# A recurrent attention layer with a feed-forward block: the list of steps after the opening rewritten in another order, transfers as they were

## The chip, the cores and the metric

The kernel runs on one core of one Trainium2 chip. The metric is the device time of one execution in microseconds (us), lower is better. The core has five engines that run side by side, each in its own order: PE (matrix multiply), DVE (vector), ACT (activations), POOL (general purpose) and SP, which here only issues transfers. An engine that waits at one instruction holds back all that stand behind it in its order.

## What is computed

For 4 batches, 8 heads, 768 positions and a head size of 48 a state of 48x48 per head is decayed and updated at each position, and read by `r`; then a normalised feed-forward block with a residual follows.

```python
for t in range(S):
    cur = np.einsum('bhd,bhe->bhde', u[None] * kt, vt)
    y[:, :, t] = np.einsum('bhd,bhde->bhe', rt, state + cur)
    state = w[None, :, :, None] * state + np.einsum('bhd,bhe->bhde', kt, vt)
...
xn = (x - mu) / np.sqrt(var + 1e-06) * g_ln        # x: y as [4, 768, 384]
out = x + np.maximum(xn @ w_ch1, 0.0) @ w_ch2      # 384 -> 1536 -> 384
```

## The kernel before

The 4x768 positions are cut into 24 chunks of 128, six to a batch, numbered 0 to 23. Inside a chunk the recurrence becomes matrix products; between chunks a state Z is carried. The feed-forward block takes chunks in groups: groups 0 to 7 hold one chunk each, groups 8 to 13 two each (chunks 8 to 19), groups 14 to 17 one each.

Nothing is scheduled by the compiler. `PLAN` (line 18) is one list of some 750 steps `name,index,engine`; the loop at its end (line 750) issues them in that order, and each engine runs its own steps in the order of the list. The letter is the engine: `v` DVE, `s` ACT, `g` POOL; `-` is PE for matrix products and SP for transfers. Waits between engines follow from which tile a step reads and writes. Buffers in PSUM are few: `hp` 2 and `at` 2 (two banks each), `y` 1 and `o` 1; a new user of one waits until the last user's reader is done.

The steps that matter, with the chunk or pair or group as index:

- `LK`, `LR`, `LV` (lines 352, 355, 358) load one chunk of k, r, v, 192 KB each, `LK2`, `LR2`, `LV2` (371, 374, 377) a pair of chunks; all are issued by SP.
- `SK`, `SR`, `SR2` multiply k and r by powers of w (through the helper at line 205) on DVE or POOL. `TRk`, `TRr` (400) transpose the result on PE, copied out by `TCk`, `TCr`; `TDk`, `TDr` (423, 428) transpose it by a transfer on SP instead. `CV2` casts v.
- `Q2` (helper, 205) multiplies the transposed tiles of a pair; `AT` (544) forms a chunk's 128x128 products per head, `AM` (553) masks them on DVE. `AT2`, `AM2` and `Y2` (504) are the same for the first four chunks.
- `S` (460 to 481) makes a chunk's share of the state and, for the first of a pair, a per-head factor in the tile `y`; `CC2` and `ZU` (565, or 205 at a batch's first chunk) read it out, `ZD` decays it, `VB2` (492) multiplies v by the factor.
- `Y` (575, 583) makes the chunk's output in the same tile `y`, from the state before, from AM and from v; `X` (590) adds `VB2`'s result. So S, ZU and CC2, Y, X take turns on one buffer.
- `SQ`, `XN`, `RS` are the normalisation. `LT` with `XT` (631, 202) transposes on PE, `LTD` (623) by a transfer on SP.
- `SW` (342 ACT, 344 DVE, 346 POOL) scales and casts one of nine pieces of the first weight, `w_f` to `w_sb`; `IW2` (349) loads the second weight on POOL's queue.
- `UP` (646) is four blocks of 128 (or two of 256) of the first feed-forward product into `hp`, `RL` (662 ACT, 664 DVE) the rectifier; `DN` (674) is a third of the second product into `o`, `OT` (730) adds the residual, `STO` (740) stores. For a one-chunk group, UP's index is 16 times the group plus the weight's third: `UP,2` needs pieces SW 6, 7 and 8.
- `DU` (279) is products of zeros for nothing, a filler of PE's time; `DU,512` is one of them.

The last chunk's second product is done in two halves (`DA`, `DB`, `OA`, `OB`, `SA`, `SB`).

Of the kernel before, what the change touches and what calls it, by code (L numbers as in the profile page):

```python
# [18 lines left out]
WF,0,s MP,1,g LK2,0,- MW,0,v ML,0,v MM2,0,g DU,3072,- UF,0,- TL,0,s MO,0,v MZ,0,v LR2,0,- LR2,1,- MP,2,g MP,0,g LK2,1,-  # L19
LN,0,s MI2,0,g MP,5,g MP,3,g WBM,0,- MP,4,g LG,0,- MM,0,g LV2,0,- DU,4096,- UWR,0,v FR2,0,s MI,0,g FR2,1,s LR2,2,- SRH,0,v  # L20
FK2,0,s SRH,1,v FK2,1,s SKH,0,v LK,5,- FK,0,s TRr,0,- SKH,1,v DU,1024,- TCr,0,s SR2,1,v TRk,0,- LR2,3,- DU,512,- SK2,1,v COL,0,-
TCk,0,s TRr,1,- LV2,1,- CV2,0,s UW,0,v Q2,0,v AT2,0,- DU,1536,- FR,0,s TCr,1,v LK,4,- WL,0,s SR2,2,g AM2,0,v S,0,- AT2,1,-
LK,6,- CC2,0,s DU,512,- ZU,0,v TRk,1,- AM2,1,v DU,512,- VB2,0,g S,1,- TCk,1,s LK,7,- DU,512,- TRr,2,- LW1,1,- SR2,3,v DU,512,-
Y2,1,- TCr,2,s LW1,2,- LV,5,- Q2,1,v Y2,0,- SK,4,g ZU,1,v UGC,0,s LV,4,- CV2,1,s X,1,v TRr,3,- SK,5,g X,0,v DU,512,-
AT2,3,- TCr,3,s DU,512,- AM2,3,v SK,7,g S,2,- XN,1,s AT2,2,- XN,0,g CC2,1,v ZU,2,v SQ,1,s DU,512,- VB2,1,g TRk,2,- AM2,2,v
S,3,- LW1,0,- TCk,2,s DU,512,- SK,6,v LT,1,- Y2,2,- SQ,0,s SW,5,g XT,1,v SW,3,s LV,6,- LT,0,- SW,4,v TRk,3,- Q2,2,g
# [6 lines left out]
DN,2,- RS,2,g LT,5,- S,7,- OT,0,v RL,66,s UP,49,- XN,6,s XT,5,v UP,50,- RL,49,v TCr,4,s LR2,6,- DN,4,- ZU,7,v UP,80,-
ZD,7,v LK,10,- CV2,4,g RL,50,v Y,7,- RL,80,s DN,5,- X,7,v LV,13,- DN,6,- Q2,4,v XN,7,s UP,65,- SQ,4,s OT,1,v LV,11,-
AT,8,- SQ,6,s SR2,6,v AT,9,- DN,8,- RS,6,s LR2,5,- AM,8,v RS,4,s DN,9,- SQ,7,s LK,11,- S,8,- DN,10,- ZU,8,v LV,10,-
UP,82,- CC2,4,s OT,2,v VB2,4,g LK,12,- LT,6,- AM,9,v Y,8,- RL,82,s DN,12,- STO,0,- RL,65,s SK,10,g DN,13,- XT,6,v LK,13,-
X,8,v DN,14,- ZD,8,g LV,12,- S,9,- UP,96,- OT,3,v SK,11,g ZU,9,v UP,98,- RL,96,s SR2,5,v Y,9,- TDk,5,- SQ,8,s DN,16,-
CV2,5,v LT,7,- TRr,5,- SK,12,v DN,17,- X,9,v TCr,5,s RL,98,v LK,15,- UP,97,- XN,9,g LK,14,- XT,7,v ZD,9,g UP,81,- RL,97,s
LR2,7,- XN,8,s SK,13,g UP,112,- RL,81,s LTD,8,- DN,18,- RS,7,s Q2,5,v TRr,6,- OT,4,v UP,114,- SK,15,g TCr,6,s RL,112,v STO,1,-
S,10,- CV2,6,g DN,20,- CC2,5,s TDk,6,- RL,114,s SK,14,v AT,10,- RS,5,s AT,11,- ZU,10,v DN,21,- SR2,7,g AM,10,v UP,113,- STO,3,-  # L40
DN,22,- AM,11,v RL,113,s TDk,7,- Y,10,- VB2,5,g UP,129,- OT,5,v TRr,7,- RL,129,s LR,19,- UP,130,- ZD,10,g X,10,v UP,133,- LV,14,-
Q2,6,v RL,130,s DN,24,- TCr,7,v STO,2,- S,12,- DN,25,- CC2,6,s LV,15,- XN,10,s VB2,6,g ZU,12,v AT,12,- SQ,9,s AT,13,- STO,5,-
AM,12,v Y,11,- RL,133,s DN,26,- Q2,7,g LK,16,- X,11,v UP,128,- OT,6,v XN,11,s Y,12,- UP,131,- X,12,v LK,17,- DN,28,- AM,13,v
SR,19,g CV2,7,s S,13,- DN,29,- LTD,9,- ZU,13,v SQ,12,s DN,30,- ZD,13,g RL,128,s Y,13,- OT,7,v AT,15,- SQ,11,s LR2,8,- AT,14,-
X,13,v UP,132,- STO,4,- SK,17,g RL,131,v SQ,13,s LR,18,- S,14,- AM,15,v LV,17,- XN,13,s DN,32,- LV,16,- XN,12,s DN,33,- ZU,14,v
# [12 lines left out]
UP,210,- AM,21,v RL,208,s DN,64,- SR,22,v S,20,- RL,210,v UP,212,- TDr,11,- CC2,10,v DN,65,- SK,22,v VB2,10,g ZU,20,v DN,66,- Y,20,-
TDk,11,- OT,16,v UP,209,- X,20,v DN,68,- RL,209,s ZD,20,v STO,14,- S,21,- XN,20,g RL,212,v CV2,11,s DN,69,- LTD,14,- ZU,21,v SQ,20,s
DN,70,- UP,213,- RS,13,s OT,17,v STO,16,- UP,211,- STO,15,- Y,21,- RL,211,s DN,72,- X,21,v DN,73,- Q2,11,v SQ,21,s AT,23,- ZD,21,v  # L60
RL,213,s AT,22,- XN,21,v S,22,- LTD,15,- UP,224,- ZU,22,v AM,22,v DN,74,- ZD,22,g RL,224,s UP,226,- CC2,11,s RS,14,s OT,18,v VB2,11,g
# [721 lines left out]
```

## Time and profile before

| | |
|---|---|
| time, median of 3 runs | 149.87 us (149.41 to 149.96) |
| span of the profiled execution, first to last instruction | 147.5 us |
| busy PE / DVE / ACT / POOL | 141.5 / 112.3 / 82.4 / 72.0 us |
| granted PE clock over the span | 1.000 |
| moved by transfers | 27.18 MB, 80338 of 85097 packets under 512 B |

The profiled execution's own time isn't listed; its span is 2.4 us less than the median of the runs, which is what lies around it (149.87 - 147.5). Matrix products are pipelined and their ends are modelled, so "busy" on PE does not mean that it lost nothing: what a product costs in a row of them is read from one start to the next. The view in order of time has, in this order, the start, the time, the engine and line, the operation, the tile written and those read, the shapes and the number of instructions merged; in brackets stands the idle time before it and what ended it. In the windows view stand the engines' busy time in each stretch, the granted clock, the share of time in which the 16 transfer engines were busy (it goes above 1 where packets overlap) and GB/s.

### The profile page before, as it was taken

Reading aid. Unit: us, or ns where it says so; the run is one execution under the profiler, and the core shown is the slowest. Engines: PE = TensorE matmul, PEld = TensorE weight load, DVE = VectorE, ACT = ScalarE, POOL = GpSimd, SP = SyncE. Lnnn points to the kernel's source line nnn. Section 1 sums busy time; section 2 is a strip of 40 time slices with the busy share of each in tenths; the row PEclk is TensorE's granted clock in tenths of the full one; section 3 lists DMA queues with packets and bytes.
Section 4 is the critical chain, followed back from the end, with each engine's and each line's share of the span. In section 5 each row is a group of like instructions: output and inputs, shape, how many; then the busy total and the mean of one; then the engine's idle time right before and its main releaser. Section 6 shows DMA issues by size and latency. Waiting matters only on the chain.

```text
span 147.5 us, 4689 instructions
## 1 busy us (share of the span) xinstructions
PE 141.5 (96%) x1943; PEld 111.1 (75%) x1943; DVE 112.3 (76%) x206; ACT 82.4 (56%) x181; POOL 72.0 (49%) x96
## 2 busy tenths in 40 slices
...
GB/s 112 300 242 240 192 339 187 283 243 215 220 95 231 202 225 165 264 205 258 164 192 196 195 235 124 173 204 227 197 112 191 182 142 154 82 46 119 8 99 111
DMA packets 85097, 27.18 MB, mean 184 GB/s; under 512 B 80338, under 2 KB 83540, under 8 KB 85076
## 3 DMA queue, kind: packets, MB, share of 16 engines
...
q8 instruction: 15, 0.25, 0.7%
...
q10 hardware_dynamic: 2, 0.00, 0.0%
HBM read 18.88 MB, written 4.72 MB: 160 GB/s over the span
## 4 chain that ended last, share of the span: by engine, by line
PE 65%; SPq 13%; DMA 11%; DVE 6%; POOL 1%; issue 1%; DVEq 0%
PE o L674 28%; PE hp L646 25%; DMA kf<-in_k_dram 6%; DMA w_f<-in_moe_w_ch_dram 5%; SPq L374 4%; SPq L352 3%; PE at L544 3%; PE y L583 2%; SPq L358 2%; PE y L481 2%; PE y L575 2%; SPq L371 1%; SPq L377 1%; DVE hT L664 1%; PE y L460 1%
## 5 line engine op out<-in xcount | busy, mean ns | idle before, releaser
L646 PE MATMUL hp<-xT,w_sb 128*128 128x128 bf16 (+1 forms) x648 | 57.1, 237 | 0.8 <-ACT w_sb L342 0.7
L662 ACT ACTIVATE hT<-hp 128x512 bf16<-128x512 f32 x55 | 32.4, 594 | 40.5 <-PE hp L646 39.7
L646 PEld LDWEIGHTS <-w_sb 128*128 128x128 bf16 x648 | 49.3, 114 | 5.1 <-ACT w_sb L342 1.3
L674 PE MATMUL o<-w_sb,hT 128*128 128x384 bf16 x276 | 53.0, 326 | 0.0
L674 PEld LDWEIGHTS <-hT 128*128 128x128 bf16 x276 | 25.0, 97 | 12.0
L553 DVE TENSOR_TENSOR A<-at,mask 128x1024 bf16<-128x1024 f32 x20 | 24.2, 1216 | 2.1 <-PE at L544 2.1
L492 POOL TENSOR_TENSOR Vb<-vf,cc 128x768 f32<-128x768 f32 x11 | 16.5, 1498 | 14.9 <-ACT cc L200 8.5
L730 DVE SCALAR_TENSOR_TENSOR ot<-o,rs,x 128x384 f32<-128x384 f32 x23 | 14.1, 615 | 12.3 <-PE o L674 7.0
L205 POOL TENSOR_TENSOR sk<-kf,Fk 128x384 bf16<-128x384 f32 x13 | 13.6, 1053 | 8.5 <-DMA kf<-in_k_dram 7.9
L597 ACT ACTIVATE sqj<-x,sm 128x384 bf16<-128x384 f32 x24 | 14.6, 609 | 2.2 <-DVE x L590 2.2
L205 POOL TENSOR_TENSOR Z<-ZS,WLZ 128x384 bf16<-128x384 f32 x8 | 8.0, 1002 | 15.4 <-DVE ZS L565 15.4
L590 DVE SCALAR_TENSOR_TENSOR x<-y,Vb 128x384 f32<-128x384 f32 x20 | 11.0, 552 | 4.5 <-PE y L583 4.1
L664 DVE TENSOR_SCALAR hT<-hp 128x512 bf16<-128x512 f32 x17 | 11.5, 684 | 3.4 <-PE hp L646 3.3
L279 PE MATMUL o<-warm 128*128 128x512 bf16 x33 | 11.3, 427 | 1.0 <-DVE warm L228 1.0
L200 ACT COPY trr<-at 128x512 bf16<-128x512 bf16 (+1 forms) x13 | 9.1, 764 | 4.4 <-PE at L400 4.4
L205 DVE TENSOR_TENSOR sr<-rf,Fr 128x768 bf16<-128x768 f32 (+1 forms) x11 | 9.5, 870 | 1.6 <-DMA rf<-in_r_dram 1.6
L205 POOL TENSOR_TENSOR sr<-rf,Fr 128x384 bf16<-128x384 f32 (+1 forms) x5 | 6.6, 1325 | 7.0 <-DMA rf<-in_r_dram 7.0
L604 ACT ACTIVATE xn<-x,sm 128x384 bf16<-128x384 f32 x13 | 7.8, 609 | 2.3 <-DVE x L590 2.3
L606 POOL TENSOR_SCALAR xn<-x,sm 128x384 bf16<-128x384 f32 x8 | 5.3, 665 | 7.6 <-DVE x L590 7.5
L205 DVE TENSOR_TENSOR q<-trk,trr 128x1024 bf16<-128x1024 bf16 x9 | 7.5, 837 | 1.4 <-ACT xn L604 1.0
L481 PE MATMUL y<-vv,sk 128*128 128x96 bf16 (+1 forms) x96 | 7.3, 204 | 0.3 <-ACT vv L200 0.2
L205 DVE TENSOR_TENSOR sk<-kf,Fk 128x384 bf16<-128x384 f32 (+1 forms) x10 | 7.4, 747 | 0.0
...
## 6 DMA issues: line engine op xcount, KB each, us to landing
...
```

What stands on the lines that cost most here:

```text
L205: engines[e].tensor_tensor(out=out, in0=in0, in1=in1, op=ALU.mult)
L279: nc.tensor.matmul(out=warm_ps[0][:].rearrange("p (a t) -> p a t", a=4), lhsT=warm[:], rhs=rhs, start=True, stop=True)
L481: nc.tensor.matmul(out=t[:, q * E2 : (q + 1) * E2].rearrange("p (e d) -> p e d", e=2), lhsT=lhs, rhs=rhs, start=first, stop=True, skip_gro ...
L492: engines[e].tensor_tensor(out=Vb2(g).rearrange("p (x h d) -> p x h d", x=2, h=H), in0=vals, in1=cc2(g)[:].unsqueeze(3).to_broadcast([P, 2 ...
L553: nc.vector.tensor_tensor(out=AA(i)[:].rearrange("p e q t -> p (e q) t"), in0=psum["at", i][:].rearrange("p e q t -> p (e q) t"), in1=mask ...
L590: nc.vector.scalar_tensor_tensor(out=xx(i)[:], in0=psum["y", i][:, :C], scalar=1.0, in1=Vb(i), op0=ALU.mult, op1=ALU.add, accum_out=sm[i][:],)
L597: nc.scalar.activation(out=sqj[:], in_=xx(i)[:], func=ACT.Square, bias=sm[i][:], scale=-float(C), accum_out=sq[g][:, j : j + 1])
L646: nc.tensor.matmul(out=t[:, a * gw : (a + 1) * gw], lhsT=w1_sb[n][kc][:, fb::FB], rhs=xT(g)[:, :size, kc, :], start=(kc == 0), stop=(kc == ...
L662: nc.scalar.activation(out=o, in_=s, func=ACT.Relu)
L664: nc.vector.tensor_relu(out=o, in_=s)
L674: nc.tensor.matmul(out=psum["o", i][:, :C], lhsT=hT(g)[:, fk, j * P : (j + 1) * P], rhs=w2_sb[d][:, a, :], start=(fk == 0), stop=(fk == FK ...
L730: nc.vector.scalar_tensor_tensor(out=ot(i)[:], in0=psum["o", i][:, :C], scalar=rs[g][:, j : j + 1], in1=xx(i)[:], op0=ALU.mult, op1=ALU.add,)
```

## The change

`PLAN` alone is changed. Its first 130 steps are the same; SP's steps come in the same order throughout. After that the same steps stand in another order, less three `DU,512`, and some change engine (number of steps in brackets):

- RL: ACT to DVE (12), DVE to ACT (10). RS: POOL to ACT (3), ACT to POOL (6). XT: DVE to ACT (4). TCk: DVE to ACT (1). TCr: ACT to DVE (1), DVE to ACT (1).
- SW: ACT to POOL (SW 2 and 8), ACT to DVE (SW 1), DVE to POOL (SW 0).
- SK: DVE to POOL (SK 8, 12, 14, 16, 22), POOL to DVE (SK 21, 23). SR: POOL to DVE (SR 19, 20), DVE to POOL (SR 18, 21). SR2: DVE to POOL (SR2 6). Q2: DVE to POOL (Q2 10).
- VB2: POOL to DVE (VB2 2, 5, 10, 11). CC2: ACT to DVE (3), DVE to ACT (2). CV2: 7 in all directions. ZD: POOL to DVE (2), DVE to POOL (2). XN: 16 in all directions.

The places of which the prediction speaks, from the diff:

```diff
-ZU,3,v DU,1024,- SW,6,s LK,8,- XT,0,v Y2,3,- SW,7,s TCk,3,v X,2,v SW,8,s AT,5,- AT,4,- X,3,v XN,2,g DU,512,- UP,2,-
-AM,5,v XN,3,s IW2,0,g LV,7,- UP,1,- RL,2,s Q2,3,g AM,4,v LT,2,- CV2,2,s DU,512,- UP,17,- RL,1,s XT,2,v S,4,- RL,17,s
...
-XT,3,v XN,5,g DU,512,- CV2,3,v LV,9,- UP,16,- RL,33,s XT,4,v SK,8,v S,6,- DN,0,- SR2,4,v CC2,3,s RL,16,s UP,48,- SQ,5,s
...
-RL,147,s OT,8,v TRr,8,- ZD,14,v UP,148,- TCr,8,s RL,145,v RL,148,v DN,36,- LK,18,- X,14,v DN,37,- CV2,8,v XN,14,s S,15,- UP,149,-
...
-SK,19,v UP,163,- SR,18,v CC2,8,s TDk,9,- UP,165,- ZU,16,v RL,163,s AM,16,v DN,41,- ZD,16,g RL,165,s DN,42,- VB2,8,g LR,21,- UP,162,-
...
-OT,12,v AT,18,- SK,20,g STO,9,- UP,180,- AM,18,v STO,11,- S,18,- SK,21,g RL,180,s UP,181,- CC2,9,v ZU,18,v DN,52,- VB2,9,g AM,19,v
-RL,181,s STO,10,- UP,179,- SQ,16,s TDk,10,- DN,53,- RL,179,s Y,18,- SQ,17,s TDr,10,- DN,54,- X,18,v UP,194,- OT,13,v UP,195,- STO,12,-
-RL,194,s LK,23,- Y,19,- SQ,14,s DN,56,- LR,23,- X,19,v SQ,15,s DN,57,- XN,18,s RS,11,g UP,197,- RL,195,s DN,58,- XN,19,s S,19,-
...
+Y2,3,- AT,5,- TCk,3,s X,2,v SW,7,s SW,6,s X,3,v SW,8,g UP,1,- RL,1,s XN,3,s CV2,2,g IW2,0,g LV,7,- AM,5,v AT,4,- UP,17,- UP,2,-
...
+DN,37,- Y,15,- UP,145,- TCr,8,v X,15,v SK,19,v RL,145,v DN,38,- S,15,- OT,9,v ZU,15,v ZD,15,v Q2,8,v AT,17,- AT,16,- AM,16,v
...
+ZU,16,v CC2,8,v VB2,8,g ZD,16,g STO,6,- LR,20,- LTD,11,- TDk,9,- LR,21,- TDr,9,- LV,19,- STO,8,- LK,20,- LK,21,- AM,17,v SR,20,v
+DN,42,- UP,160,- RL,160,s UP,179,- Y,16,- OT,10,v RL,179,s UP,181,- UP,162,- DN,44,- DN,45,- X,16,v Q2,9,v Y,17,- X,17,v XN,17,v
+CV2,9,g XN,16,s RL,162,s SQ,13,s RS,10,g DN,46,- UP,165,- OT,11,v SK,21,v AT,18,- AT,19,- AM,19,v S,18,- RL,165,s RL,181,s
+CC2,9,s UP,177,- UP,178,- DN,48,- DN,49,- DN,50,- RL,177,v AM,18,v VB2,9,g SK,20,g ZU,18,v UP,180,- RL,180,s SQ,15,s RL,178,s
+OT,12,v Y,19,- X,19,v SR,21,g LTD,12,- STO,9,- STO,11,- STO,10,- TDk,10,- TDr,10,- DN,52,- UP,176,- Y,18,- DN,53,- UP,197,-
```

More of the change, by code (lines that the diff above doesn't have):

```diff
@@ L18 @@
 PLAN = """
[L19 to L26, printed above, removed]
-ZU,3,v DU,1024,- SW,6,s LK,8,- XT,0,v Y2,3,- SW,7,s TCk,3,v X,2,v SW,8,s AT,5,- AT,4,- X,3,v XN,2,g DU,512,- UP,2,-
@@ L33 @@
[L33 to L45, printed above, removed]
@@ L58 @@
[L58 to L61, printed above, removed]
@@ L66 @@
-SB,23,- OA,23,v SA,23,-
+WF,0,s MP,1,g LK2,0,- MW,0,v ML,0,v MM2,0,g DU,3072,- UF,0,- TL,0,s MO,0,v MZ,0,v LR2,0,- LR2,1,- MP,2,g MP,0,g LK2,1,- LN,0,s
+MI2,0,g MP,5,g MP,3,g WBM,0,- MP,4,g LG,0,- MM,0,g LV2,0,- DU,4096,- UWR,0,v FR2,0,s MI,0,g FR2,1,s LR2,2,- SRH,0,v FK2,0,s
+SRH,1,v FK2,1,s SKH,0,v LK,5,- FK,0,s TRr,0,- SKH,1,v DU,1024,- TCr,0,s SR2,1,v TRk,0,- LR2,3,- DU,512,- SK2,1,v COL,0,- TCk,0,s
+TRr,1,- LV2,1,- CV2,0,s UW,0,v Q2,0,v AT2,0,- DU,1536,- FR,0,s TCr,1,v LK,4,- WL,0,s SR2,2,g AM2,0,v S,0,- AT2,1,- LK,6,-
@@ new lines @@
+CC2,0,s DU,512,- ZU,0,v TRk,1,- AM2,1,v DU,512,- VB2,0,g S,1,- TCk,1,s LK,7,- DU,512,- TRr,2,- LW1,1,- SR2,3,v DU,512,- Y2,1,-
+TCr,2,s LW1,2,- LV,5,- Q2,1,v Y2,0,- SK,4,g ZU,1,v UGC,0,s LV,4,- CV2,1,s X,1,v TRr,3,- SK,5,g X,0,v DU,512,- AT2,3,- TCr,3,s
+DU,512,- AM2,3,v SK,7,g S,2,- XN,1,s AT2,2,- XN,0,g CC2,1,v ZU,2,v SQ,1,s DU,512,- VB2,1,g TRk,2,- AM2,2,v S,3,- LW1,0,- TCk,2,s
+DU,512,- SK,6,v LT,1,- Y2,2,- SQ,0,s SW,5,g XT,1,v SW,3,s LV,6,- LT,0,- SW,4,v TRk,3,- Q2,2,g ZU,3,v DU,1024,- LK,8,- XT,0,v
@@ new lines @@
+Y2,3,- AT,5,- TCk,3,s X,2,v SW,7,s SW,6,s X,3,v SW,8,g UP,1,- RL,1,s XN,3,s CV2,2,g IW2,0,g LV,7,- AM,5,v AT,4,- UP,17,- UP,2,-
+AM,4,v SW,2,g SW,0,g LR2,4,- LK,9,- IW2,1,g IW2,2,g XN,2,s LT,3,- S,4,- LT,2,- XT,3,v CC2,2,v ZU,4,v SW,1,v Q2,3,g SK,8,g RL,2,s
+RL,17,s XT,2,s UP,49,- RL,49,s SQ,2,s AT,7,- AT,6,- UP,34,- UP,33,- Y,4,- RL,34,s RL,33,s VB2,2,v X,4,v UP,16,- UP,0,- RL,16,s
+RL,0,s LV,8,- LV,9,- Y,5,- UP,32,- RL,32,s XN,4,s AM,7,v X,5,v AM,6,v XN,5,v RS,1,g SK,9,g CV2,3,s UP,48,- DN,0,- RL,48,s
@@ new lines @@
+SR2,4,v UP,50,- LT,4,- LT,5,- S,6,- UP,18,- ZU,6,v XT,4,s RS,0,s RL,50,v CC2,3,s TRr,4,- RL,18,s TCr,4,s Y,6,- DN,1,- UP,64,-
+VB2,3,v X,6,v XT,5,v RL,64,v XN,6,s RS,2,s SQ,3,s DN,2,- S,7,- OT,0,v UP,66,- UP,80,- TDk,4,- LR2,6,- LK,10,- LV,13,- LV,11,-
+LR2,5,- LK,11,- LV,10,- LK,12,- STO,0,- LK,13,- LV,12,- ZU,7,v DN,4,- Y,7,- SQ,4,s LT,6,- DN,5,- RS,3,s RL,80,s XT,6,s DN,6,-
+RL,66,v UP,81,- X,7,v CV2,4,v OT,1,v Q2,4,v ZD,7,v XN,7,g AT,8,- AT,9,- DN,8,- UP,97,- RL,81,s AM,9,v S,8,- ZU,8,v AM,8,v DN,9,-
@@ new lines @@
+LT,7,- SQ,6,s CC2,4,s UP,82,- DN,10,- Y,8,- SR2,6,g VB2,4,g OT,2,v SK,10,g ZD,8,v SK,11,g X,8,v SR2,5,v XT,7,s RL,82,s RL,97,s
+TRr,6,- UP,65,- DN,12,- UP,96,- TDk,5,- LK,15,- LK,14,- RL,96,v RL,65,v DN,13,- DN,14,- S,9,- ZU,9,v SQ,7,s RS,7,g RS,6,g RS,4,g
+ZD,9,g SK,12,g CV2,6,g TRr,5,- UP,98,- Y,9,- OT,3,v RL,98,v TCr,5,s XN,8,s SK,13,g X,9,v CV2,5,v UP,112,- DN,16,- UP,114,-
+DN,17,- SK,15,g SK,14,g Q2,5,v XN,9,s RL,112,s TCr,6,s DN,18,- S,10,- UP,113,- RL,113,s SQ,8,s RL,114,s OT,4,v ZU,10,v CC2,5,v
@@ new lines @@
+AT,10,- AM,10,v VB2,5,v AT,11,- LR2,7,- LTD,8,- STO,1,- TDk,6,- STO,3,- TDk,7,- DN,20,- DN,21,- DN,22,- SR2,7,g UP,128,- SQ,5,s
+RS,5,s RL,128,s Y,10,- OT,5,v X,10,v Q2,6,v UP,132,- DN,24,- TRr,7,- UP,130,- S,12,- XN,10,g ZD,10,g RL,132,s RL,130,s CC2,6,s
+TCr,7,s LR,19,- LV,14,- STO,2,- LV,15,- STO,5,- AM,11,v ZU,12,v UP,131,- DN,25,- Y,11,- DN,26,- X,11,v AT,13,- AT,12,- OT,6,v
+VB2,6,g XN,11,s S,13,- UP,133,- RL,131,s RL,133,s LK,16,- LK,17,- LTD,9,- LR2,8,- DN,28,- DN,29,- DN,30,- SR,19,v ZU,13,v
@@ new lines @@
+ZD,13,g Q2,7,g CV2,7,g AM,12,v AM,13,v Y,12,- X,12,v OT,7,v UP,129,- AT,14,- AT,15,- XN,12,g SQ,9,s RS,8,g SK,16,g SK,17,g
+RL,129,s UP,147,- UP,149,- Y,13,- DN,32,- DN,33,- AM,14,v RL,147,v X,13,v SQ,10,s RL,149,s XN,13,s STO,4,- LR,18,- LV,17,-
+LV,16,- LTD,10,- TDk,8,- LK,18,- LK,19,- LV,18,- STO,7,- LV,20,- UP,146,- RL,146,s S,14,- DN,34,- CC2,7,s VB2,7,g SR,18,g
+UP,148,- SR2,8,v AM,15,v TRr,8,- UP,144,- OT,8,v ZU,14,v RL,148,v ZD,14,g SQ,12,s RL,144,v DN,36,- Y,14,- X,14,v UP,161,-
+DN,37,- Y,15,- UP,145,- TCr,8,v X,15,v SK,19,v RL,145,v DN,38,- S,15,- OT,9,v ZU,15,v ZD,15,v Q2,8,v AT,17,- AT,16,- AM,16,v
```

28 lines of the change are left out of this document (14 added, 14 removed).

## The prediction

> **What bounds the kernel now.** I read the page first, then the windows, then PE in order of time, then who waits on the transfers.
>
> ```profile
> span 147.5 us, 4689 instructions
> ...
> PE 141.5 (96%) x1943; PEld 111.1 (75%) x1943; DVE 112.3 (76%) x206; ACT 82.4 (56%) x181; POOL 72.0 (49%) x96
> ```
>
> ```profile
> 44.00:60.00 16.00, 16.00 (x230) 12.90 (x228) 13.82 (x26) 9.69 (x25) 7.08 (x8) 1.00 1.04 204
> 60.00:77.00 17.00, 17.00 (x244) 13.59 (x242) 15.73 (x27) 10.44 (x25) 12.32 (x10) 1.00 1.03 216
> ```
>
> The span is 147.5, and 149.87 - 147.5 = 2.4 us lie around it in the median of the runs; I take these as unchanged. PE is busy in every microsecond of the two windows, at a granted clock of 1.00. DVE is close behind (15.73 of 17), and the transfer engines stand at 1.04 and 1.03. So PE bounds, with two others near it: a gain can only be PE time that is no use or PE time lost between products, and it can be given back to DVE or to the transfers.
>
> Where PE loses time is read from its starts:
>
> ```profile
> 25.67 0.39 PE L279 MATMUL o<-warm 128*128 128x512 bf16 x1
> 26.10 0.25 PE L646 MATMUL hp<-xT,w_sb 128*128 128x128 bf16 x1
> 26.71 0.25 PE L646 MATMUL hp<-xT,w_sb 128*128 128x128 bf16 x1 [0.37 <-ACT w_sb L342]
> 27.33 1.42 PE L646 MATMUL hp<-xT,w_sb 128*128 128x128 bf16 x22 [0.36 <-ACT w_sb L342]
> 28.58 0.33 PE L631 MATMUL at<-ident,xn 128*128 128x128 bf16 x3
> 28.75 0.38 PE L279 MATMUL o<-warm 128*128 128x512 bf16 x1
> 28.97 0.83 PE L646 MATMUL hp<-xT,w_sb 128*128 128x128 bf16 x12
> 29.64 0.34 PE L460 MATMUL y<-uwI,q 128*128 128x2 bf16 x8
> ...
> 35.27 0.38 PE L279 MATMUL o<-warm 128*128 128x512 bf16 x1
> 35.48 0.83 PE L646 MATMUL hp<-xT,w_sb 128*128 128x128 bf16 x12
> ...
> 81.66 1.47 PE L674 MATMUL o<-w_sb,hT 128*128 128x384 bf16 x8
> 83.21 0.35 PE L481 MATMUL y<-vv,sk 128*128 128x96 bf16 x4
> ```
>
> In the chain that ended last, the same products in an unbroken run:
>
> ```profile
> 103.75 0.20 PE y L583 x8
> 103.95 0.65 PE o L674 x4
> 104.60 1.31 PE hp L646 x12
> ```
>
> One UP of a single chunk costs 29.64 - 28.97 = 0.67, one DN 0.65, one UP of two chunks 1.31 / 2 = 0.66, a Y without a state 0.20.
>
> **The start.** Three fillers go: 26.10 - 25.67, 28.97 - 28.75 and 35.48 - 35.27 are 0.43 + 0.22 + 0.21 = 0.86. UP2 and UP1 run from 26.10 to 28.58, 2.48 for 2 x 0.67 = 1.34 of work: 1.14 lost to the weight pieces SW6 to SW8 on ACT. In the new list UP1 and UP17 go ahead of UP2, SW8 moves to POOL, and TCk3 goes to ACT ahead of the pieces. UP1 needs only pieces that come earlier. What is late next is SW8, behind Q2,2 on POOL:
>
> ```profile
> 21.03 1.48 POOL L492 TENSOR_TENSOR Vb<-vf,cc 128x768 f32<-128x768 f32 x1
> 23.44 0.97 POOL L346 TENSOR_SCALAR w_sb<-w_f,g_neg 128x512 bf16<-128x512 f32 x1 [0.94 <-DMA w_f<-in_moe_w_ch_dram]
> 24.39 2.12 POOL L205 TENSOR_TENSOR q<-trk,trr 128x1024 bf16<-128x1024 bf16 x1
> ```
>
> 24.39 + 2.12 + 0.97 = 27.5. PE comes to UP2 at 26.10 - 0.43 + 1.34 = 27.0 and needs that piece two products later, so it still waits about 0.4. Queued behind SW8 on POOL are CV2,2 and the second weight's loads; DN0, which needs the first of those, comes only after ten UPs (10 x 0.67 = 6.7), and that is the cover. Net at the start: 0.86 + 1.14 - 0.4 = 1.6.
>
> **The middle.** S15 loses 83.21 - 81.66 - 2 x 0.65 = 0.25, waiting for X14 to free the tile `y`. In the new order it follows Y15, with UP145 and DN38 between, so X15 has 0.66 + 0.65 = 1.3 to be done in, and the 0.25 goes. What is late next there is DVE's queue, which TCr8 joins just ahead of X15; X14, TCr8 and X15 have from Y14 to S15 all of UP161, DN37, UP145 and DN38, 2.6, and that is the cover. That makes 1.85; waits of about a tenth each elsewhere I leave out. The moves of RL, XT, XN, CC2, CV2 and ZD between engines I cost at nothing where PE's order leaves at least an UP's 0.66 between a step and its user, which it mostly does; the exception is below. If PE waits nowhere else, the time is 149.87 - 1.85 = 148.0.
>
> **Where it can be given back.** In the new list Y19 stands ahead of Y18, and DVE runs Q2,9, X17, XN17, OT11, SK21, AM19, RL177, AM18, ZU18 before it. SK21 used to be POOL's; now all of DVE stands behind it while k of chunk 21 is on its way. Its users in that queue: Y19 needs AM19 and the `y` tile that ZU18 sets free, UP180 needs RL177, DN52 needs OT12 behind ZU18. The rows:
>
> ```profile
> 97.25 0.91 DVE L205 TENSOR_TENSOR q<-trk,trr 128x1024 bf16<-128x1024 bf16 x1 [0.32 <-DMA trr<-sr]
> 98.08 0.54 DVE L205 TENSOR_TENSOR sr<-rf,Fr 128x384 bf16<-128x384 f32 x1
> 98.55 0.68 DVE L664 TENSOR_SCALAR hT<-hp 128x512 bf16<-128x512 f32 x1
> 99.15 1.37 DVE L202 CAST vv<-vf 128x768 bf16<-128x768 f32 x1
> 100.44 0.60 DVE L730 SCALAR_TENSOR_TENSOR ot<-o,rs,x 128x384 f32<-128x384 f32 x1
> 100.97 1.21 DVE L553 TENSOR_TENSOR A<-at,mask 128x1024 bf16<-128x1024 f32 x1
> 102.10 0.16 DVE L202 COPY cc<-y 128x16 f32<-128x16 f32 x1
> 102.18 0.54 DVE L205 TENSOR_TENSOR Z<-y,WLZ 128x384 bf16<-128x384 f32 x1
> ```
>
> ```profile
> 99.11 2.28 POOL L205 TENSOR_TENSOR sk<-kf,Fk 128x384 bf16<-128x384 f32 x2 [1.48 <-DMA kf<-in_k_dram]
> ```
>
> ```profile
> 105.75 0.33 PE L575 MATMUL y<-Z,trr 128*128 128x96 bf16 x4
> ```
>
> From start to start, a multiplication of this shape takes 98.55 - 98.08 = 0.47, an RL 0.60, an AM 1.13; ZU18 ends 0.54 after its start. From the landing of k 21 to Y19: 0.47 + 1.13 + 0.60 + 1.13 + 0.54 = 3.9. Before, SK20 and SK21 ended at 99.11 + 2.28 = 101.4, and POOL had waited for the data; the second can have begun at 100.2 and no sooner than its k landed, so I put the landing at 100.1. PE came to Y19 at 105.75; the new list does 3 DN, 3 two-chunk UPs and one short Y less before it (by counting steps): 3 x 0.65 + 3 x 0.66 + 0.20 = 4.1. Unhindered, PE comes to it at 105.75 - 4.1 - 1.85 = 99.8. With k 21 landing x earlier than before, Y19 starts at 104.0 - x at the soonest; the gain left is 1.85 - (4.2 - x) = x - 2.4, at most 1.85. All hangs on x.
>
> SP issues in order, and before it stood still here:
>
> ```profile
> 87.09 1.31 SPq L623 DMA_TRANSPOSE xT<-xn  x1
> 89.87 1.23 SPq L423 DMA_TRANSPOSE trk<-sk  x1
> ```
>
> ```profile
> 90.00:91.00 1.00, 1.00 (x10) 0.89 (x9) 1.00 (x3) 0.69 (x2) 0.25 (x1) 1.00 0.00 0
> ```
>
> LTD11 ended its issue at 87.09 + 1.31 = 88.4, TDk9 came at 89.87: 1.4 of waiting, for SK19 on DVE, and the transfer engines ran dry (0.00 from 90 to 91). Before, DVE did XN15, OT9, AM17 and RL160 between X15 and SK19; in the new list SK19 comes straight after X15, so that this wait goes. The rest of x is PE's lead of 1.85, for the transfers that wait for computed tiles (LTD10, TDk8) follow PE. Bounds of x: 0, if the transfers are paced by themselves (1.03 busy from 60 to 77), and 1.85 + 1.4 = 3.3 or a little more, if SP fills its pauses. I take 3.2, near the upper end, because of the empty row at 90. Gain 0.8.
>
> POOL takes over 5 SKs and a Q2, among others, and gives off 4 VB2s and 2 SKs. Whether that hurts DVE, this row bears on:
>
> ```profile
> 21.33 1.59 DVE L205 TENSOR_TENSOR sk<-kf,Fk 128x384 bf16<-128x384 f32 x1
> ```
>
> A multiplication that takes 0.54 at 98.08 took 1.59 here, while POOL's VB2 ran to 21.03 + 1.48 = 22.5; and the cast at 99.15 took 1.37 beside POOL's two multiplications. In the new list SK21 falls beside VB2,9 and SK20 on POOL. The added cost lies between 0 and 1.59 - 0.54 = 1.05; I take 0.1, since SK21 starts after VB2,9 by my times and may come ahead of SK20. Forecast: 149.87 - 0.8 + 0.1 = 149.2. The Trainium skill, "SBUF — State Buffer", section "Who interferes with whom", says that a DVE instruction with two SBUF inputs and a GpSimd instruction that reads SBUF exclude each other for the whole of the one that began first; the row at 21.33 agrees, and by that rule the sum would be up to 1.05 worse at this place, if POOL comes first.
>
> **The rivals.**
>
> Transfers do not move up. They stood at 1.04 and 1.03 while PE was full, so an earlier issue may only lengthen the queue. With x = 1, PE waits at Y19 for 4.2 - 1.0 = 3.2 and the time is 149.87 + 1.4 = 151.3. It is slower by over 0.5% (0.75 us, about what a measurement of this kernel can tell from no change) when x is below 1.6. Against it: the empty row at 90.
>
> PE never waits after the start. If k 21 lands 4.2 sooner, through pauses that I have not counted, 148.0 stands, and somewhat less if the waits of a tenth that I left out go too. Against it: x needs 0.9 more than the pauses that I found.
>
> POOL holds DVE. SK21 comes just after SK20 has begun and waits for it: 0.95 more than forecast (1.05 for the 0.1 that I took), 150.1. It is the rule above as a mechanism of this place.
>
> That the list does not do what it says can be left out: by the diff the two hold the same steps but for three fillers.
>
> **How the numbers follow.** The forecast, 149.2 with a range of its own of 148.5 to 149.9 (x from 2.4 to 3.8), gets 0.45: every term but x is read directly. Never waiting gets 0.20, transfers that don't move up 0.21, POOL's hold 0.14. Faster by over 0.5% is below 149.12: 0.20 and half of 0.45, 0.43 together. Slower by over 0.5% is above 150.62: 0.21 and a little of POOL's hold, 0.24. Within: 0.33. The range goes from 147.6 to 151.3, leaving out the ends of both outer cases.
>
> **What would show it.** Right: no filler after 24 us, UP2 short of its last piece by half a microsecond at most, S15 without its 0.25; DVE idle ahead of a multiplication `sk<-kf` near 96, with k as the releaser, and PE pausing before Y19 for about a microsecond; no pause of SP ahead of TDk9. Wrong: no such idle time and PE unbroken to the end (the second rival); a pause of over 2.5 us there, or SP's loads landing where they did (the first); that multiplication lasting over 1 us beside POOL (the third); or a new wait in a place that I haven't named.

## The result, and the profile after

Before, on this chip: 149.92 us median of 4 runs (149.41 to 150.3). After: 154.0 us median of 4 (152.3 to 157.12). The ratio is 1.0289, 95% interval 1.0217 to 1.0361: slower by 2.9%. The profiled execution of after took 154.26, with a span of 152.5. Some executions of any version are disturbed, with a lower clock or a longer opening: the ratios in this document leave them out, the medians do not, and as the profiles of a_dve4, a_loads, b_loads, a_fit and a_half_l are of such executions, no wait ahead of 60 us and no absolute time is taken from those five.

The head of the page of after: span, busy time of each engine, and the chain that ended last.

```profile
span 152.5 us, 4672 instructions
...
PE 142.0 (93%) x1940; PEld 111.0 (73%) x1940; DVE 115.3 (76%) x205; ACT 79.2 (52%) x171; POOL 82.9 (54%) x107
...
PE 46%; DMA 21%; DVE 10%; POOL 9%; issue 5%; SPq 5%; ACT 0%; DVEq 0%; POOLq 0%
```

PE has 0.5 us more busy time (142.0 for 141.5) in a span that is 5.0 longer. So PE waits, and in the last chain 21% is transfers. The waits of PE in after, by what released it (us in total, times, longest):

```profile
PE o L674 <- DVE ot L730: 1.8, 2, 1.3
PE at L544 <- DMA trk<-sk: 1.2, 1, 1.2
...
PE y L575 <- DVE Z L205: 0.8, 1, 0.8
PE hp L646 <- DVE hT L664: 0.8, 1, 0.8
PE y L460 <- DVE ZS L565: 0.6, 1, 0.6
PE hp L646 <- POOL w_sb L346: 0.6, 1, 0.6
```

Most releasers are DVE, though DVE is idle for a quarter of the span. DVE in order of time shows what it stands waiting for; the bracket is the idle time before the instruction and what ended it:

```profile
87.56 0.56 DVE L205 TENSOR_TENSOR sk<-kf,Fk 128x384 bf16<-128x384 f32 x1 [1.63 <-DMA kf<-in_k_dram]
88.04 0.68 DVE L664 TENSOR_SCALAR hT<-hp 128x512 bf16<-128x512 f32 x1
88.64 0.61 DVE L730 SCALAR_TENSOR_TENSOR ot<-o,rs,x 128x384 f32<-128x384 f32 x1
...
100.33 1.34 DVE L205 TENSOR_TENSOR sk<-kf,Fk 128x384 bf16<-128x384 f32 x1 [1.64 <-DMA kf<-in_k_dram]
101.60 1.21 DVE L553 TENSOR_TENSOR A<-at,mask 128x1024 bf16<-128x1024 f32 x1
102.73 0.68 DVE L664 TENSOR_SCALAR hT<-hp 128x512 bf16<-128x512 f32 x1
...
114.79 0.56 DVE L205 TENSOR_TENSOR sr<-rf,Fr 128x384 bf16<-128x384 f32 x1 [1.43 <-DMA rf<-in_r_dram]
115.26 0.55 DVE L565 TENSOR_TENSOR ZS<-y,Z 128x384 f32<-128x384 f32 x1
```

These are SK19, SK21 and SR22. Ahead of each DVE stands idle until the load has landed, and among the steps right behind it is one that PE waits for: OT9 (`ot`) for DN40, RL177 (`hT`) for UP180, ZU19 (`ZS`) for S20. PE itself, at the place that the prediction named:

```profile
100.59 2.12 PE L674 MATMUL o<-w_sb,hT 128*128 128x384 bf16 x12
103.46 0.82 PE L646 MATMUL hp<-xT,w_sb 128*128 128x256 bf16 x6 [0.76 <-DVE hT L664]
105.06 0.33 PE L575 MATMUL y<-Z,trr 128*128 128x96 bf16 x4 [0.78 <-DVE Z L205]
```

The next table gives what PE lost at each place: from the start of the product before it to its own start, less what that step takes elsewhere. So UP180 comes 2.87 after DN48 to DN50 began (103.46 - 100.59), for three DN of 0.65: 0.92. An empty cell is a wait of under 0.15. The last row holds all places after 24 us, those not listed too (1.52 at Y5 in a_half, 0.60 at S10 in a_k21), the fillers not counted; many small gaps are in it, so its differences count, to some tenths.

| PE waits at | for | before | after | a_k21 | a_half_e | a_half |
|---|---|---|---|---|---|---|
| UP2, UP1 | weight pieces | 1.14 | | | | |
| UP16 | SW0 on POOL | | 0.71 | 0.54 | | |
| AT8 | transpose of k 8, 9 | | 1.36 | 1.64 | | |
| DN24 | OT5, which waits for store 1 | | 0.76 | 0.52 | | |
| DN40 | k 19 | | 1.44 | 2.12 | 1.92 | 0.49 |
| UP180, Y19, DN52 | k 21 | | 2.01 | 0 | 2.02 | 0 |
| S20 | r 22 | | 0.78 | 2.44 | 1.71 | 0.57 |
| S21, Y20 | Z steps on POOL and DVE behind v 21 | | 0.70 | 0.50 | 0.49 | 0.69 |
| all places | | 3.2 | 9.5 | 9.7 | 8.5 | 5.4 |

9.5 - 3.2 = 6.3 more lost, less the 0.86 of the fillers that are gone, is 5.4; the span grew by 5.0. So the waits hold the whole loss.

### The profile page after: what moved, and what is told of

It reads as the page before. It is cut to its first block, busy times and chain, and to the rows that moved or that the text cites. A ratio compares the mean times of both kernels' runs of the same rounds, so it can differ in the third digit from the quotient of the medians.

```text
span 152.5 us, 4672 instructions
## 1 busy us (share of the span) xinstructions
PE 142.0 (93%) x1940; PEld 111.0 (73%) x1940; DVE 115.3 (76%) x205; ACT 79.2 (52%) x171; POOL 82.9 (54%) x107
## 4 chain that ended last, share of the span: by engine, by line
PE 46%; DMA 21%; DVE 10%; POOL 9%; issue 5%; SPq 5%; ACT 0%; DVEq 0%; POOLq 0%
PE o L674 17%; PE hp L646 14%; DMA kf<-in_k_dram 10%; POOL sk L205 3%; DMA rf<-in_r_dram 3%; DMA out_dram<-ot 3%; DMA trk<-sk 3%; PE hp L504 2%; SPq L358 2%; DMA vf<-in_v_dram 2%; PE at L400 2%; DVE hT L664 2%; PE y L481 2%; PE o L279 2%; PE at L544 1%
## 5 line engine op out<-in xcount | busy, mean ns | idle before, releaser
L205 POOL TENSOR_TENSOR sk<-kf,Fk 128x384 bf16<-128x384 f32 x16 | 17.2, 1087 | 6.9 <-DMA kf<-in_k_dram 6.9
L205 POOL TENSOR_TENSOR sr<-rf,Fr 128x768 bf16<-128x768 f32 (+1 forms) x6 | 9.5, 1589 | 10.1 <-DMA rf<-in_r_dram 10.1
L492 POOL TENSOR_TENSOR Vb<-vf,cc 128x768 f32<-128x768 f32 x7 | 10.3, 1477 | 6.6 <-DVE cc L202 5.5
L664 DVE TENSOR_SCALAR hT<-hp 128x512 bf16<-128x512 f32 x19 | 12.8, 683 | 1.3 <-PE hp L646 1.3
L616 POOL TENSOR_SCALAR rs<-sq 128x1 f32<-128x1 f32 (+1 forms) x11 | 2.9, 261 | 18.5 <-ACT sqj L597 17.8
L205 DVE TENSOR_TENSOR sr<-rf,Fr 128x384 bf16<-128x384 f32 (+1 forms) x10 | 9.8, 985 | 3.2 <-DMA rf<-in_r_dram 3.2
L205 POOL TENSOR_TENSOR q<-trk,trr 128x1024 bf16<-128x1024 bf16 x4 | 8.7, 2174 | 3.7 <-PE hp L646 3.7
L604 ACT ACTIVATE xn<-x,sm 128x384 bf16<-128x384 f32 x11 | 6.6, 613 | 3.5 <-DVE x L590 3.5
L202 POOL CAST vv<-vf 128x768 bf16<-128x768 f32 x6 | 5.4, 898 | 5.4 <-DMA vf<-in_v_dram 5.4
L565 DVE TENSOR_TENSOR ZS<-y,Z 128x384 f32<-128x384 f32 x12 | 6.6, 551 | 2.2 <-POOL Z L205 2.1
```

The source lines that it names most:

```text
L205: engines[e].tensor_tensor(out=out, in0=in0, in1=in1, op=ALU.mult)
L492: engines[e].tensor_tensor(out=Vb2(g).rearrange("p (x h d) -> p x h d", x=2, h=H), in0=vals, in1=cc2(g)[:].unsqueeze(3).to_broadcast([P, 2 ...
L664: nc.vector.tensor_relu(out=o, in_=s)
```

## The experiments

The theory at first: DVE's queue is held, because steps that wait for loads were put on it. Its main rival: PE's order and the engines chosen lose time by themselves, whatever the loads do. From the fifth run on the question was what makes the loads late: SP's fixed order (theory L) or the pace of the transfers (theory T), and in the end in which stretch. Each run was compared with runs of the kernel before on the same chip. The chips differ from row to row, so it is the ratios that are compared below:

| kernel | median us (runs) | ratio to before, 95% interval |
|---|---|---|
| a_noload | 147.27 (4) | 0.9891 [0.9819, 0.9963] |
| b_noload | 148.38 (10) | 0.9955 [0.9908, 1.0002] |
| a_dve4 | 158.78 (4) | 1.0615 [1.0526, 1.0705] |
| b_start | 149.04 (10) | 0.9991 [0.9938, 1.0044] |
| a_k21 | 154.26 (4) | 1.0323 [1.0259, 1.0387] |
| a_ot5 | 156.83 (4), profiled one 154.14 | none taken |
| a_loads | 151.29 (10) | 1.0094 [1.0045, 1.0142] |
| b_loads | 151.39 (5) | 1.0133 [1.0063, 1.0202] |
| a_fit | 150.76 (7) | 1.011 [1.0052, 1.0167] |
| a_k17 | 155.46 (4) | 1.0441 [1.0371, 1.0512] |
| a_half | 148.99 (10) | 1.0043 [0.9988, 1.0097] |
| b_half | 148.35 (10) | 0.9974 [0.9932, 1.0017] |
| a_half_e | 153.93 (4) | 1.0281 [1.0196, 1.0366] |
| a_half_l | 150.66 (10) | 1.0061 [1.002, 1.0102] |

**Without the later loads** (a_noload from after, b_noload from before).

```diff
-LK,8 to LK,23; LV,10 to LV,23; LR2,4 to LR2,8; all LR
```

> The new list without the loads of k for chunks 8 to 23, of v for chunks 10 to 23 and of r for chunks 8 to 23 (stale chunks are used in their place, so the output is not the reference's); stores, weights and transposing transfers stay. If the new list loses its time to loads that land too late (in whichever queue the wait stands), PE is nearly unbroken here and the time is 146.5 to 148.5. If the placement itself is at fault (POOL has 10.9 us more to do, 82.9 against 72.0), most of the loss stays: 151 to 154.

> The list of before without the same loads (same part left out). PE was nearly unbroken already, so both theories expect 148.5 to 149.9. What counts is the difference to the new list without loads: new list faster by 1 to 2.5 us if loads are the cause, slower by 2 or more if the placement is.

Without these loads the new list is not the slower one: 147.27 for 148.38, though with four executions of a_noload and intervals that overlap, the 1.1 us between them may be less or nothing. With the loads it is 2.9% slower. So neither PE's order nor the engines chosen lose the time by themselves, and that rival falls. By the ratios the loads cost the list of before 1 - 0.9955 = 0.4%, or 0.7 us, and that of after 1.0289 - 0.9891 = 4.0%, or 6.0 us.

**Four steps out of DVE's way** (a_dve4).

```diff
-SR,19,v ahead of ZU,13   SK,21,v ahead of AM,19   SK,19,v behind X,15    SR,22,v ahead of ZU,19
+SR,19,g behind VB2,6     SK,21,g behind SK,20     SK,19,v behind AM,16   SR,22,v behind AM,21
```

> The new list with four multiplications on loaded tiles taken out of DVE's way: SR19 and SK21 back to POOL, SK19 behind AM16 and SR22 behind AM21 on DVE. Theory A, DVE's queue is held by loads: PE's waits at DN40 (1.4), UP180 and Y19 (1.9) and S20 (0.8) go, 154.0 falls by 3 to 4.5 to 149.5 to 151. Theory B, the loads' own pace holds PE: its waits turn up at other places behind the same loads, 153 to 154.5.

It went the other way, to 1.0615 where after has 1.0289. DVE and then SP, in order of time:

```profile
124.51 1.21 DVE L552 TENSOR_TENSOR A<-at,mask 128x1024 bf16<-128x1024 f32 x1
125.64 0.55 DVE L204 TENSOR_TENSOR sr<-rf,Fr 128x384 bf16<-128x384 f32 x1
```

```profile
118.89 1.15 SPq L357 DMA_DIRECT2D vf<-in_v_dram  x2
126.33 1.23 SPq L427 DMA_TRANSPOSE trr<-sr  x1
127.66 1.28 SPq L422 DMA_TRANSPOSE trk<-sk  x1
```

SR22 now waits behind AM21 instead of for its load, and SP stands from 120.04 to 126.33 until SR22 has made the tile that TDr11 transposes; PE then waits 1.92 for TDk11, which SP issues right behind TDr11. A step that waits for a load could not simply go later here, since a transpose in SP's queue needs it. The waits at DN40 and UP180 are gone from this profile; others have come behind the same stream of loads: 2.4 in two places, S18 and S20, for POOL's cast of v, which itself stood until v had landed, and 1.4 for a transpose. That is the sign of theory B, in a time that neither theory expected. So taking these steps out of DVE's way in this manner does not undo the loss, and the first theory falls in this form.

**The start alone** (b_start: the new order and engines from step 130 to SP's load LR2,4, in the list of before).

```diff
-...Y2,3,- SW,7,s TCk,3,v X,2,v SW,8,s AT,5,- AT,4,- X,3,v XN,2,g DU,512,- UP,2,- ... UP,1,- ... UP,17,-
+...Y2,3,- AT,5,- TCk,3,s X,2,v SW,7,s SW,6,s X,3,v SW,8,g UP,1,- ... UP,17,- UP,2,-
```

> The list of before with the new start alone: three fillers gone, UP1 and UP17 ahead of UP2, SW8 on POOL, TCk3 ahead on ACT. If the 1.6 us that the prediction gave the start are real and stay, 148.0 to 148.7. If PE's lead is taken back by loads that do not move up, 149.3 to 150.0.

No difference that can be measured: 1.6 us would have been a ratio of 0.989, below the interval. The waits of PE in b_start up to 44 us:

```profile
28.97 0.33 PE L480 MATMUL y<-vv,sk 128*128 128x96 bf16 x4 [0.87 <-ACT vv L199]
...
40.52 0.81 PE L673 MATMUL o<-w_sb,hT 128*128 128x384 bf16 x4 [0.52 <-DMA w_sb<-in_moe_w_ch_dram]
43.80 0.81 PE L673 MATMUL o<-w_sb,hT 128*128 128x384 bf16 x4 [0.79 <-DVE ot L729]
```

PE comes to DN2 sooner and meets the second weight's load, and DN4 meets its `ot`: 0.87 + 0.52 + 0.79 = 2.2 new waits take the 1.6 back. (This execution took 150.24, the median 149.04, so that others may lose less.)

**k 21 alone earlier** (a_k21).

```diff
-TDk,9,- LR,21,- TDr,9,- LV,19,- STO,8,- LK,20,- LK,21,-
+TDk,9,- LK,21,- TDr,9,- LV,19,- STO,8,- LK,20,- LR,21,-
```

> The kernel after, with one exchange in SP's order: the load of k for chunk 21 goes to the place of the load of r for chunk 21 (91.2 us), and that one to its place (95.4). Theory L (loads come late because SP issues in one fixed order, and PE waits wherever DVE or POOL wait for them): k21 lands near 96 instead of 100.3, SK21 on DVE loses its wait of 1.64 us, and the PE waits around UP180, Y19 and DN52 (0.92 + 0.94 + 0.15) fall to 0.5 or less: 1.5 us less, 152.5 us where after has 154.0. Theory T (the transfers' pace is the bound, whatever their order): others land as much later, and the time stays within 0.5 us of after. The prediction's own formula, gain lost = 2.4 - x with x = 4, would make the whole 2.0 us come back.

DVE of a_k21, in order of time:

```profile
98.31 0.61 DVE L729 SCALAR_TENSOR_TENSOR ot<-o,rs,x 128x384 f32<-128x384 f32 x1
98.84 0.55 DVE L204 TENSOR_TENSOR sk<-kf,Fk 128x384 bf16<-128x384 f32 x1
99.31 1.22 DVE L552 TENSOR_TENSOR A<-at,mask 128x1024 bf16<-128x1024 f32 x1
...
113.90 1.32 DVE L204 TENSOR_TENSOR sr<-rf,Fr 128x384 bf16<-128x384 f32 x1 [2.32 <-DMA rf<-in_r_dram]
```

SK21 runs without a wait and 1.5 sooner than in after, and the three waits at UP180, Y19 and DN52 are gone (2.01 to 0 in the table). At SR22 DVE then waits 2.32 instead of 1.43, S20's wait goes from 0.78 to 2.44, and the time is that of after. The place that I had named is real; clearing it alone buys nothing.

Why S20 gains nothing is worth following. SP issues the load of r 22 behind LTD13, which waits for a tile of XN18. That came sooner here, and the load was issued at 109.12 for 111.43 in after, 2.3 sooner; but it landed 4.8 behind its issue instead of 3.4, so SR22 began only 0.89 sooner. Then SR22 took 1.32 instead of 0.56, beside a multiplication on POOL that had begun 0.08 ahead of it:

```profile
113.82 0.99 POOL L204 TENSOR_TENSOR sr<-rf,Fr 128x384 bf16<-128x384 f32 x1
```

ZU19, which S20 waits for, began 0.11 sooner than in after (115.15 for 115.26). So of the 2.3 us the transfers took 1.4 and POOL's hold on DVE 0.8.

**One more output tile** (a_ot5).

```diff
-'x': 12, ... 'ot': 4
+'x': 11, ... 'ot': 5
```

> The kernel after with 5 output tiles in place of 4 (and 11 tiles of x in place of 12, which no step waits for). OT5 no longer waits 1.15 us for the landing of store 1, so PE's wait of 0.76 us between UP132 and DN24 goes. Theory L: 0.7 us less than after, 153.3; Theory T: no change, since the next load decides in its place (DN40 waits 0.7 longer).

DN24's wait goes; the profiled execution has 154.14 for 154.26, and S20 still waits 0.87. The other three took 156.58 to 157.37, so that this run shows no gain, and no more than that.

**Five loads moved up** (a_loads, b_loads). The expectations count seven; by the diff LK18, LK19, LK21, LV21 and LR22 go up, and LR21, TDk8 and LTD13 go back.

```diff
+LK,18 and LK,19 ahead of TDk,8;  LV,21 and LR,22 ahead of LTD,13;  LK,21 and LR,21 exchanged;  'x': 11, 'ot': 5
```

> The kernel after with seven loads earlier in SP's order and nothing else moved: k21 exchanged with r21; k18 and k19 ahead of the transpose of k of chunks 16 and 17 (2 us earlier); v21 and r22 ahead of the transpose LTD13 (3.7 us earlier, in a pause of SP); 5 output tiles for 4. Theory L: the PE waits at DN40 (1.44), UP180 to DN52 (2.0), S20 and S21 (1.14) and DN24 (0.76) fall from 5.3 us to about 1: 149.6 us, level with before. Theory T: 153 to 154, the waits move to the steps whose transfers are pushed back.

> The kernel before with the same seven loads moved and 5 output tiles for 4. PE waits for no load there after 43 us in the trace, so by either theory it stays within 0.5 us of before; slower by 1 us or more would say that the moved loads push back the transposes, which would count against a_loads too.

Taken together the moves bring the ratio from 1.029 to 1.009, about two thirds of the loss; their own profile has no wait left at DN40, DN24 or UP180 to DN52, and 0.19 at S20, but a new one of 2.0 at UP147, which waits for the transpose LTD9. Before gets slower by the same moves, by 1.3%, which neither theory expected. One place of the price shows in DVE of b_loads:

```profile
104.90 0.86 DVE L204 TENSOR_TENSOR sr<-rf,Fr 128x384 bf16<-128x384 f32 x1 [1.86 <-DMA rf<-in_r_dram]
```

This is SR21, whose load was exchanged with that of k 21 and now comes late; the cast CV2,9 stands two steps behind it, and PE loses 0.77 at S18 waiting for that cast. The rest of the 1.3% was not traced. So L holds in part, and its price is visible.

**PE's list fitted to a landing** (a_fit: a_loads with DN8 and DN9 ahead of AT8 and LT7 behind DN10).

```diff
-AT,8,- AT,9,- DN,8,- UP,97,- ... S,8,- ... DN,9,- LT,7,- ... UP,82,- DN,10,-
+DN,8,- DN,9,- AT,8,- AT,9,- UP,97,- ... S,8,- ... UP,82,- DN,10,- LT,7,-
```

> The kernel after with the seven loads moved earlier and 5 output tiles, and PE's list fitted to one landing that can't be moved: DN8 and DN9 stand ahead of AT8, which waits for the transpose of k of chunks 8 and 9 (1.36 us in the trace of after), and LT7 behind DN10. Theory L (PE stands where its list asks for a tile before its transfer has landed): the wait at AT8 falls below 0.3 us, and the time is 1 us under the one with the loads moved alone (151.3 median, about 150.4 among its undisturbed runs): 149.5, level with before. Theory T (the transfers' pace sets the end): no change, 150.4.

1.011 for 1.0094: nothing gained, as T expected; whether AT8's wait went is not shown, since it lies ahead of 60 us. No version with all its loads beats before.

**SP's feeders earlier** (a_k17).

```diff
-ZD,13,g Q2,7,g CV2,7,g ... XN,12,g RS,8,g SK,16,g SK,17,g
+ZD,13,g SK,16,g SK,17,g ... XN,12,g Q2,7,g CV2,7,g ... RS,8,g
```

> The kernel after with SK16, SK17 and XN12 ahead of Q2,7 and CV2,7 on POOL, no load moved. It tests why k21 did not move up: the transposes LTD10 and TDk8, which wait for XN12 and SK17, hold SP. Theory L: SP issues TDk8 near 80.0 instead of 80.96, k18 and k19 land 1 us earlier, PE's wait at DN40 falls from 1.44 to about 0.5, and k21 comes up to 1 us earlier; of that S20, which waits for r22, takes most back, so the time falls by 0.5 us at most, 153.5. Theory E (POOL's added work is the bound): Q2,7 is 2 us later, S14 waits, 154.5 or more.

Slower still. SP in a_k17:

```profile
75.48 4.07 SPq L357 DMA_DIRECT2D vf<-in_v_dram  x2
79.82 1.24 SPq L622 DMA_TRANSPOSE xT<-xn  x1
81.56 1.24 SPq L422 DMA_TRANSPOSE trk<-sk  x1
```

The tile for TDk8 was ready 4 us sooner, and TDk8 is issued at 81.56, no sooner than in after (80.96): SP spent 4.07 us on the two loads ahead. They took 3.79 in after and 1.80 before. SP was not held here by the computed tile but by its own transfers. The time is in the range of theory E, but its sign, a wait at S14, is not in the profile. That it is 1.5% slower than after I can't put down to one place: S10 lost 1.37 and S20 1.67 in its profile, and S10 stands ahead of the steps that were moved, so that its wait is not theirs.

**Half the bytes** (a_half, b_half). Each load fetches `H // 2`, four of the eight heads; the expectation of a_half says three of six.

```diff
-queues[e].dma_start(out=kf(i), in_=chunk_src(k, i))
+h = H // 2 if i >= 8 else H; queues[e].dma_start(out=kf(i)[:, :h], in_=chunk_src(k, i)[:, :h])
```

> The kernel after, in which each load of k from chunk 8, of v from chunk 10 and of r from chunk 8 on fetches three of the six heads, so half the bytes and packets, with as many transfers, issued in the same order at the same places (the other half of each tile keeps what an earlier chunk left there, and the output is not the reference's). Theory L in the form that SP's order and its waits for computed tiles make the loads late: the loads land about as late, 152.5 or more. Theory T (the pace of the 16 DMA engines makes them late): most of what the whole loads cost comes back, 148 to 149.5, near the 147.3 without any.

> The same halved loads in the kernel before (output not the reference's either). Both theories: between 148.4, as without those loads, and 149.6, so at most 1 us less than before. If the new list keeps its 1.1 us lead over the old one with half the loads, a_half is under this.

With the same transfers at the same places of SP's order, half the bytes bring back 1.0289 - 1.0043 = 2.5 of the 4.0 points that the loads cost, 3.7 of the 6.0 us. b_half came out at 148.35, at the edge of what was expected; a_half is not under it, so with half the loads the new list still has no lead. Loads of k land in 2.9 us, where whole ones take 4.3 (the median from issue to landing, last column; after, whose 20 include four of the opening, then a_half):

```profile
kf<-in_k_dram SPq DMA_DIRECT2D x20, 192.0 KB, 4.3
```

```profile
kf<-in_k_dram SPq DMA_DIRECT2D x16, 96.0 KB, 2.9
```

The windows of after, then of a_half (stretch, its length, busy PE, PEld, DVE, ACT, POOL, the clock, the transfers' share, GB/s):

```profile
84.00:96.00 12.00, 10.75 (x125) 8.81 (x124) 10.34 (x21) 6.31 (x14) 4.63 (x5) 1.00 0.97 201
96.00:108.00 12.00, 10.46 (x122) 7.96 (x121) 8.62 (x17) 4.22 (x11) 6.29 (x7) 1.00 0.83 195
```

```profile
84.00:96.00 12.00, 11.70 (x141) 9.53 (x139) 10.85 (x22) 7.04 (x17) 5.41 (x7) 1.00 0.76 170
96.00:108.00 12.00, 12.00 (x142) 9.38 (x141) 9.53 (x17) 5.21 (x12) 6.75 (x7) 1.00 0.84 155
```

From 84 to 96 PE fills again, and the transfers' share falls from 0.97 to 0.76. From 96 to 108 the share is the same in both (0.83 and 0.84), and PE is full all the same: SK21 runs at 96.85 without a wait, 3.5 sooner than in after.

Halving changes two things at once. A load lands sooner after its issue, and SP is done sooner with issuing: the eight loads from LR2,6 to LK12 hold it for 8.55 us in after (43.57 to 52.12) and for 4.43 in a_half (38.86 to 43.29). So the load of k 21 is issued at 92.3 instead of 95.43 and lands 2.8 behind that instead of 4.9. What makes the loads late is then mostly the transfers' own pace, with what it costs SP counted in. Bytes and packets were halved together; which of the two sets the pace is not shown.

**Which stretch** (a_half_e, a_half_l: half the bytes in one stretch only).

```diff
-h = H // 2 if i >= 8 else H            (k; r and v alike)
+h = H // 2 if 8 <= i <= 15 else H      (a_half_e: loads issued up to 59 us)
+h = H // 2 if i >= 16 else H           (a_half_l: loads issued from 65 us on)
```

> The kernel after with half the bytes in the loads that SP issues up to 59 us alone (k of chunks 8 to 15, v of 10 to 13, r of 8 to 15, three of six heads each; the output is not the reference's); all later loads whole. Halving all of them gave 149.0 against 154.0. Theory T-early (the new list outruns the transfers in its first stretch, and what follows is that lag handed on): 150 or less. Theory T-late (each stretch has its own late loads; the lag of the first is taken back at S20, which waits for r22 at 114.8 us): only what is early returns and the last late load takes it back, so 152.5 to 153.5.

> The kernel after with half the bytes in the loads that SP issues from 65 us on alone (k from chunk 16, v from 14, r from 16; output not the reference's). Theory T-early: the lag of the first stretch stays, 152.5 or more. Theory T-late: k19, k21 and r22 land in time, so the waits at DN40, UP180 to DN52 and S20 (1.44 + 2.0 + 0.78) mostly go, 150.5, and what stays is the 3 us lost up to 66 us.

Clear for T-late over T-early, though 153.93 lies 0.4 above the range that T-late gave. With the early half relieved, AT8, UP16 and DN24 no longer wait, and the time is that of after: the waits at DN40 and S20 have grown instead. DVE in a_half_e, then POOL:

```profile
86.36 0.56 DVE L204 TENSOR_TENSOR sk<-kf,Fk 128x384 bf16<-128x384 f32 x1 [2.12 <-DMA kf<-in_k_dram]
...
113.67 1.41 DVE L204 TENSOR_TENSOR sr<-rf,Fr 128x384 bf16<-128x384 f32 x1 [1.50 <-DMA rf<-in_r_dram]
```

```profile
113.66 0.99 POOL L204 TENSOR_TENSOR sr<-rf,Fr 128x384 bf16<-128x384 f32 x1
```

With the late half relieved, 150.66, a ratio of 1.0061. So the late stretch decides, and what PE gains ahead of it turns into a longer wait there. That the landing alone takes it back is not shown: in a_half_e r 22 landed 1.1 sooner than in after, and it was SR22, 1.41 long beside POOL, that gave 0.85 of it away again (ZU19 began at 114.99 for 115.26). No run took POOL's hold away. In a_noload SR22 took 1.15 too, and S20 lost no time: the hold is paid where DVE is late already.

## Why the prediction was wrong

The forecast was 149.2, the measured time 154.0, outside the range and on the other side of the time before.

- **The start: right in itself, worth nothing.** No filler is left, UP2 and UP1 no longer lose 1.14, and S15 follows without its 0.25. I counted it as gain to the end. b_start shows that even in the list of before it is taken back within 18 us. The 0.4 that I left for UP2 did not come; UP16 lost 0.71 in its place, for SW0, which had moved to POOL.
- **The step that failed: "x took 3.2".** I put k 21's landing at 100.1 before and expected it 3.2 earlier; SK21 was released at 100.33, so x was -0.2. The pause of SP ahead of TDk9 did go, as I had said (LTD11's issue ends at 89.58, TDk9 comes at 89.69), but SP reached it 1.2 later than before, so TDk9 came at the same time (89.69 for 89.87). SP in after:

```profile
74.81 3.79 SPq L358 DMA_DIRECT2D vf<-in_v_dram  x2
...
88.24 1.34 SPq L623 DMA_TRANSPOSE xT<-xn  x1
89.69 1.44 SPq L423 DMA_TRANSPOSE trk<-sk  x1
```

  Two loads of v took 3.79 to issue where before took 1.80, and the tile of TDk8, from SK17, was done only at 80.94; TDk8 came at 80.96, 1.24 later than before, and what followed came as much later. LK21 was even issued sooner (95.43 for 96.59) and landed no sooner. "Transfers do not move up" was the first rival, and it held, at a higher price than its 151.3. I weighed one empty microsecond against shares of 1.03 and 1.04 over 33 us, and took the microsecond.
- **POOL's hold, 0.1: mis-sized, by 0.7.** SK21 took 1.34 beside POOL's VB2,9, against 0.55 in a_k21, where it ran ahead of VB2,9; the third rival, at the same place. With x = -0.2 my own sum has Y19 at 104.2, plus 0.8 for the hold 105.0; it started at 105.06. The chain was right, its input wrong: x - 2.4 = -2.6, and with the hold the sum would have been 149.87 + 2.6 + 0.8 = 153.3.
- **"PE waits nowhere else": wrong.** I looked for one late load and found the middle one of three. S20 too stands earlier in the new list, with 2 DN and 4 UP less ahead of it (by counting steps, 2 x 0.65 + 4 x 0.66 = 3.9 us), while SP's order is the same; I had not counted there. S20, S21 and Y20, behind r 22 and v 21, add 0.78 + 0.36 + 0.34 = 1.5 after Y19; with 153.3 that is 154.8, where the profiled execution took 154.26. UP16, AT8 and DN24 (2.8 together) lie ahead of Y19 and cost nothing of their own at the end: a_half_e took them away and gained nothing.
- **The moves "costed at nothing": right for the end.** In a_noload all of them are there, and it is not slower than b_noload. The time lies in the loads that DVE and POOL wait for, not in the engines chosen.

Shown: the loads make the whole loss, their pace most of it, and the late stretch decides. Shown only in part: which transfers SP's order should have moved; a_loads recovers two thirds, and of what b_loads lost by the same moves 0.77 us was traced to a place. Open: how much POOL's hold on DVE adds; it took 0.8 at SK21 and as much at SR22 in a_k21 and a_half_e, and no run was made without it.
